# Attention and a routed expert layer on one core: new costs in the planner that orders the merge, and another path for two weight remainders

## The chip, the cores and the metric

The kernel runs on one core of one Trainium2 chip. The metric is the device time of one execution in microseconds (us). Engines are named as in the profile: PE multiplies matrices, DVE and ACT work on vectors, POOL issues the indirect and the adding transfers, SP issues plain transfers.

## The reference

Windowed attention (8 batches, 8 heads, 576 positions, head size 64, window 64) gives 4608 tokens of 512 numbers. Tokens are then assigned greedily to 8 experts of at most 576 tokens each, by all token-expert scores in falling order, and every expert is a two-layer product:

```python
logits = x @ w_gate
for idx in np.argsort(-logits.flatten()):
    tok, e = (int(idx) // E, int(idx) % E)
    if assigned[tok] >= 0 or counts[e] >= cap:
        continue
    assigned[tok] = e
    counts[e] += 1
...
    h = np.maximum(x[mask] @ w1[e], 0.0)
    out[mask] = h @ w2[e]
```

## The kernel before, in words

The first part, up to about 150 us, is the attention (`attention`), which writes the tokens `xs` to HBM and the gate scores to `L`. The change does not touch it.

The second part, the merge, runs two chains side by side. **Routing** (`Routing.steps`, L536) goes through the experts one after the other. A pass for expert p makes every token's best choice (`choices`, L490, six DVE operations), copies the choices on ACT into `one4` (L557), searches the score of the last token that still fits in 8 rounds (DVE compares L514, a count on PE L593, then some ten small DVE operations L602 to L663), and writes the list of the expert's tokens (L704 to L774: scan, PE products L707 and L756 and L768, the index tile `idx` L774). After the list, DVE updates the state for the next pass (L779 to L807). **Products** (`Experts.steps`, L984) are PE's bulk: for each expert a first layer (L1021), of 16 units with 12 matmuls, and a second (L1054 and L1064). Numbers are split in a rounded part and a remainder, so a matrix product takes three matmuls (wh by xh, wl by xh, wh by xl).

Between the two stands `turn` (L938): as soon as `idx` of expert p is there, POOL issues five gathers (L957; four of 128 tokens, one of 64) into `xg`, and PE transposes the tiles (L975) into two PSUM buffers; ACT copies each to `xh` (L946), DVE makes the remainder `xl` (L950) and frees the buffer. A transposed expert can start its first layer.

Weights come in eight chunks of 512 KB per expert (`load`, L865): SP (for the first expert's last four chunks POOL, L877) fetches a chunk into `st`; ACT rounds it to `wh` (L900). The remainder `wl` is made either by a DVE subtraction (L906; `quick`, L931: the first expert's chunks 0, 1, 2 and the last weights of all), or by an ACT copy of -wh (L911) and an adding transfer that POOL issues (L913), which adds `st` onto it.

The order of the instructions on each engine is not written by hand. `Streams` (L1072) is a planner that runs when the program is built: every chain is a generator that issues instructions and yields the time after which it may go on. `busy(dt, eng)` (L1084) books time on an engine and returns when the booking ends. What is issued first in planned time stands first in the engine's queue, and an engine takes its queue in order. So a wrong cost shows as an engine waiting for another. The costs of the DVE chain are booked by

```python
def dve(self, dt):
    return self.busy(0.4 * dt, "dve") + 0.6 * dt
```

so 40% of a step occupies DVE. ACT isn't booked at all. The transposes of expert p are planned from the gathers: `there` = now + POOL's booking (6400 ns) + GATHER, 2900 ns for the first expert and 6500 ns for the others, and tiles (0, 1), (2, 3), (4) come 3840, 1280 and 0 ns before it; from the third expert on they also wait for the next counting product of the routing, or at most JOIN ns. In the first round of a pass, PE's count waits 3500 ns of planned time after the ACT copies (L558).

Of the kernel before, what the change touches and what calls it, by code (L numbers as in the profile page):

```python
# [10 lines left out]
FT = mybir.dt.float32  # L11
# [5 lines left out]
OP = mybir.AluOpType  # L17
# [381 lines left out]
class Routing:  # L399
# [132 lines left out]
    def dve(self, dt):  # L532

        return self.busy(0.4 * dt, "dve") + 0.6 * dt

    def steps(self, p):  # L536
# [7 lines left out]
        if p < E - 1:  # L544
# [19 lines left out]
            for r in range(NR):  # L564
# [4 lines left out]
                if not p:  # L569
# [8 lines left out]
                    yield self.dve(1350)  # L578
                else:
                    c4 = self.room(128, 72)  # L580
                    cn, c4 = c4[:, 64:72], c4[0:M, 0:4 * ND]
                    for j0, j1 in ((0, 20), (20, 36)):
                        self.compare(G, thr, j0, j1)
                        yield self.dve(420)
                    for f in rest:
                        f()
                    yield self.dve(200) + slack
# [18 lines left out]
                    yield self.dve(450)  # L606
# [4 lines left out]
                    yield self.dve(400)  # L611

                step = float(1 << 28 - 4 * r) if r else 1.0
                if own:
# [4 lines left out]
                    yield self.dve(400)  # L619
# [5 lines left out]
                    yield self.dve(400) + slack  # L625
# [41 lines left out]
                yield self.dve(400)  # L667
            for f in rest:
                f()
            yield self.dve(200)  # L670
# [11 lines left out]
            yield self.dve(600)  # L682
# [8 lines left out]
            yield self.dve(600)  # L691
        else:
# [7 lines left out]
            yield self.dve(800)  # L700
# [4 lines left out]
        yield self.dve(250) + (600 if p else 0)  # L705
# [7 lines left out]
                                       op0=OP.add, op1=OP.mult)  # L713
        si = tile_([128, 3, NJ], I32, name="si")
        nc.vector.scalar_tensor_tensor(si[:, 0], Y[:, 0], -1.0, Y[:, 1], op0=OP.add, op1=OP.add)
        yield self.dve(500)
# [4 lines left out]
        yield self.dve(500)  # L721
# [18 lines left out]
        yield self.dve(410)  # L740
        nc.scalar.activation(Rw[:, 0], pairs(A_), AF.Copy, scale=self.lane)
        if p:
            nc.vector.tensor_tensor(Bw, pairs(self.r32), sb[:, 1].rearrange("p (q h) -> p q h", h=2)[:, None]
                                    .to_broadcast([128, 32, NJ // 2, 2]), OP.is_equal)
            yield self.dve(1200)
        for j0, j1 in ((0, NJ),) if p else ((0, 18), (18, 36)):
# [5 lines left out]
            yield self.dve(600) + slack + (500 if p else 0)  # L752
# [7 lines left out]
            yield self.busy(n * (18 if p else 29) + (90 if p else 0))  # L760
        yield self.dve(200) + slack
        ils = tile_([72, 32, 2], BF, name="ils")
        nc.vector.tensor_copy(ils.rearrange("p a h -> p (a h)"), il[0:72])
        yield self.dve(300)
# [7 lines left out]
        yield self.busy(100) + 200 + slack  # L772
        idx = self.rt.tile([128, 5], U32, name=f"idx{p}")
        nc.vector.tensor_copy(idx, ip)  # L774
        self.idx[p] = idx
        yield self.dve(200)
        if p < E - 1:
            if not p:
                nc.vector.scalar_tensor_tensor(self.eid, m, T[:, 0:1], best, op0=OP.is_gt, op1=OP.mult)  # L779
            eq = tile_([128, NJ], FT, name="eq")  # L780
            nc.vector.scalar_tensor_tensor(eq, Y[:, 1], CAP + 0.5, X[:, 1], op0=OP.is_lt, op1=OP.mult)
            nc.vector.scalar_tensor_tensor(self.eid, eq, code[:, 0:1], self.eid, op0=OP.mult, op1=OP.add)
            nc.vector.tensor_scalar(self.un, self.eid, 0.0, None, op0=OP.is_equal)
            yield self.dve(400)
            e1 = tile_([128, E], FT, name="e1")
            nc.vector.tensor_scalar(e1, self.cw, code, -FAR, op0=OP.is_equal, op1=OP.mult)
            nc.vector.tensor_tensor(V, V, e1[:, None, :].to_broadcast([128, NJ, E]), OP.add)
            yield self.dve(600)

            nc.vector.scalar_tensor_tensor(self.oh, m[:, :, None].to_broadcast([128, NJ, E]), T[:, 0:1], one,  # L790
                                           op0=OP.is_gt, op1=OP.mult)
            c2 = tile_([128, E], BF, name="c2")
            with nc.allow_low_precision(reason="whole numbers up to 36"):
                nc.vector.tensor_reduce(c2, self.oh.rearrange("p j e -> p e j"), axis=AX.X, op=OP.add)
            e2 = tile_([128, E], FT, name="e2")
            nc.vector.tensor_scalar(e2, self.cw, code, -1.0e6, op0=OP.is_equal, op1=OP.mult)
            nc.vector.tensor_tensor(self.left, self.left, e2, OP.add)
            if 0 < p < E - 2:
                self.kept = c2
                yield self.dve(1100)  # L800
                return
            yield self.dve(1100) + (slack if p < OWN else 1500)
            cn = self.room(128, E)
            nc.tensor.matmul(cn, self.ones, c2, start=True, stop=True)
            self.joined()
            yield self.busy(110) + 200 + slack
            nc.vector.tensor_tensor(self.left, self.left, cn, OP.add)  # L807
            yield self.dve(200)
# [21 lines left out]
class Experts:  # L830
# [34 lines left out]
    def load(self, p, ei):  # L865
# [26 lines left out]
        for i in range(2 * NCH):  # L892
# [8 lines left out]
            yield 1050  # L901
# [3 lines left out]
            if quick:  # L905
                nc.vector.tensor_tensor(lo, st[i], hi.bitcast(FT), OP.subtract)  # L906
                dt = self.busy(1130, "dve")
                self.spawn(self.ready(p, i, hi, lo), dt + 300 if p else 0)
            else:

                nc.scalar.activation(lo, hi.bitcast(FT), AF.Copy, scale=-1.0)  # L911
                yield 1150
# [18 lines left out]
    def quick(self, p, i):  # L931
        return p == 0 and i < 3 or p * 2 * NCH + i >= (E - 2) * 2 * NCH + NCH
# [5 lines left out]
    def turn(self, p, idx):  # L938
# [4 lines left out]
        def evac(a, n, t):  # L943
# [4 lines left out]
            yield 700  # L948
# [6 lines left out]
        for a in range(5):  # L955
# [3 lines left out]
            self.busy(TOKENS, "dma")  # L959
        self.gathered += 1  # L960
        there = self.clock() + self.busy(6400, "pool") + GATHER[p > 0]
# [4 lines left out]
        for tiles in ((0, 1), (2, 3), (4,)) if p else ((0,), (1,), (2,), (3,), (4,)):  # L966
            yield max(0, there - 1280 * (4 - tiles[-1]) - self.clock())
            if p > 1:

                n0, t0 = self.joins, self.clock() + JOIN[tiles[0] // 2]  # L970
                yield lambda: self.routed or self.joins > n0 or self.clock() >= t0
            for n, a in enumerate(tiles):
# [3 lines left out]
                dt = self.busy(260)  # L976
# [7 lines left out]
    def steps(self, p, idx):  # L984
# [6 lines left out]
        def evac(f, c0, h):  # L991
            c1 = c0 + h.shape[1]
            nc.scalar.activation(hh[:, f, c0:c1], h, AF.Relu)  # L993
            yield 500
# [34 lines left out]
        self.first += 1  # L1029

        def put(a, o):
            ot = fw.tile([128, DM], FT, name="ot", bufs=3)
            m = 128 if a < 4 else 64
            if a < 4:
                nc.scalar.activation(ot, o, AF.Copy)  # L1035
            else:
                t = fw.tile([64, DM], FT, name="low")
                nc.scalar.activation(t, o[64:128], AF.Copy)
                yield 650
# [67 lines left out]
def body(tc, q, k, v, vt, wg, w1, w2, xs, out):  # L1107
    nc = tc.nc
    with ExitStack() as ctx:
# [17 lines left out]
        def route():  # L1127
            for p in range(E):
                for dt in rt.steps(p):
# [3 lines left out]
                    if p in rt.idx and p not in listed:  # L1133
                        listed.add(p)
                        st.add(ex.turn(p, rt.idx[p]))
                    yield dt
            ex.routed = True
# [6 lines left out]
        known, listed = set(), set()  # L1144
# [20 lines left out]
```

## Time and profile before

| | us |
|---|---|
| median of 3 runs (lowest, highest) | 650.95 (649.75, 651.98) |
| the profiled execution, its own time | 650.87 |
| its span, first to last instruction | 648.9 |
| PE busy (share of the span) | 611.3 (94%) |
| DVE busy | 454.1 (70%) |
| ACT busy | 346.1 (53%) |
| POOL busy | 186.2 (29%) |

The page's slices show the attention up to about 150 us, a stretch with PE nearly idle around 150 to 180 us (the first routing pass, with no product to cover it), and then PE at 9 or more tenths up to the end. Where an engine's row carries a bracket, it gives the idle time before the instruction and what ended it. PEclk is the granted share of TensorE's full clock of 2.4 GHz; 0.5 is 1.2 GHz.

### The profile page before, as it was taken

To read this page: it belongs to the slowest core of one execution; us is meant where nothing else is said; L and a number is where in the kernel's file an instruction comes from. 1 tells how busy PE (TensorE), PEld (TensorE's weight loads), DVE (VectorE), ACT (ScalarE), POOL (GpSimd) and SP (SyncE) were. 2 spreads that over 40 slices of the span, in tenths; PEclk is the share of its full clock that TensorE was granted. 3 is DMA by queue.
4 is the path that set the end of the run, shared out by engine and by line. 5 is a ranking of instruction groups with operands and counts; after the bars stand their busy time and mean duration, and the time that the engine had idled before them with its cause. 6 is when DMAs were issued, how large, how long until landed. Compare 5 with 4: busy or idle time off the path is not lost.

```text
span 648.9 us, 16904 instructions
## 1 busy us (share of the span) xinstructions
PE 611.3 (94%) x6375; PEld 532.0 (82%) x6375; DVE 454.1 (70%) x2126; ACT 346.1 (53%) x724; POOL 186.2 (29%) x242
## 2 busy tenths in 40 slices
PE   8899999994599999999899999999999999999996
PEld 6677778884389879978797898899789879989985
DVE  7788888886789868876786787688678755523300
ACT  6798999980265176337526643572664354524210
POOL 1334353331141162026105411620541164011011
PEclk9999999996599998999899999999999999999999
DMA  9999999931376199459918964991896399411001
GB/s 313 373 367 368 371 385 368 336 109 36 130 237 130 30 315 240 82 195 218 234 21 300 246 120 149 247 242 30 295 248 122 124 273 321 153 36 38 1 25 48
DMA packets 44657, 127.81 MB, mean 197 GB/s; under 512 B 4632, under 2 KB 5272, under 8 KB 44576
## 3 DMA queue, kind: packets, MB, share of 16 engines
q1 hardware_dynamic: 30736, 79.52, 34.1%
q0 software_dynamic: 13552, 46.69, 30.8%
q8 instruction: 50, 0.82, 0.5%
q10 hardware_dynamic: 288, 0.52, 0.3%
q14 instruction: 31, 0.25, 0.1%
HBM read 82.15 MB, written 18.87 MB: 156 GB/s over the span
## 4 chain that ended last, share of the span: by engine, by line
PE 49%; issue 20%; POOL 4%; DMA 2%; ACT 1%; DVE 0%; POOLq 0%; ACTq 0%
PE h L1021 22%; PE o L1064 18%; PE o L1054 3%; POOL out L1043 2%; PE rps L593 2%; DMA wl<-st 1%; PE tp L975 1%; POOL xg L957 1%; DMA xg<-xs,idx 1%; POOL wl L913 1%; PE rps L756 1%; ACT wh L900 0%; ACT wl L911 0%; PE rps L758 0%; POOLq L1161 0%
## 5 line engine op out<-in xcount | busy, mean ns | idle before, releaser
L1043 POOL DMA_INDIRECT out<-ot,idx x40 | 40.4, 1010 | 252.8 <-ACT ot L1035 87.8
L993 ACT ACTIVATE hh<-h 128x256 fp32r<-128x256 f32 (+1 forms) x128 | 52.4, 409 | 110.3 <-PE h L1021 109.0
L1064 PE MATMUL o<-wh,hh 128*128 128x512 f32 x256 | 101.4, 396 | 0.0
L1064 PE MATMUL o<-wh,hl 128*128 128x512 f32 x256 | 100.8, 394 | 0.0
L1064 PE MATMUL o<-wl,hh 128*128 128x512 f32 x256 | 100.5, 393 | 0.0
L141 ACT ACTIVATE pe<-st,mx 128x128 f32<-128x128 f32 x288 | 92.0, 393 | 5.8 <-DVE mx L136 5.5
L1021 PE MATMUL h<-xh,wh 128*128 128x256 f32 (+1 forms) x512 | 93.0, 302 | 1.7 <-issue 0.9
L1021 PE MATMUL h<-xl,wh 128*128 128x256 f32 (+1 forms) x512 | 93.4, 300 | 0.0
L998 DVE SCALAR_TENSOR_TENSOR hl<-h,hh 128x256 fp32r<-128x256 f32 x128 | 53.6, 419 | 56.5 <-ACT hh L993 55.9
L1021 PE MATMUL h<-xh,wl 128*128 128x256 f32 (+1 forms) x512 | 91.9, 299 | 0.0
L1021 PEld LDWEIGHTS h<-xh,wh 128*128 128x128 f32 x512 | 76.8, 192 | 2.8 <-ACT xh L946 1.4
L1021 PEld LDWEIGHTS h<-xh,wl 128*128 128x128 f32 x512 | 76.7, 192 | 0.0
L1021 PEld LDWEIGHTS h<-xl,wh 128*128 128x128 f32 x512 | 76.6, 192 | 0.0
L900 ACT ACTIVATE wh<-st 128x1024 fp32r<-128x1024 f32 x64 | 67.3, 1052 | 2.7 <-DMA st<-w 2.5
L136 DVE CUSTOM_DVE_ANT_0 st<-Sp,mask 128x128 f32<-128x128 f32 x288 | 63.7, 285 | 5.7 <-PE Sp L128 5.2
L913 POOL DMA_DIRECT2D wl<-st x49 | 44.6, 976 | 68.9 <-ACT wl L911 25.9
L1035 ACT ACTIVATE ot<-o 128x512 f32<-128x512 f32 x32 | 19.1, 597 | 70.9 <-PE o L1064 63.2
L1064 PEld LDWEIGHTS o<-wh,hl 128*128 128x128 f32 x256 | 48.1, 188 | 9.6
L1064 PEld LDWEIGHTS o<-wl,hh 128*128 128x128 f32 x256 | 48.1, 188 | 9.3
L1064 PEld LDWEIGHTS o<-wh,hh 128*128 128x128 f32 x256 | 48.1, 188 | 9.3
L911 ACT ACTIVATE wl<-wh 128x1024 fp32r<-128x1024 f32 x49 | 51.8, 1056 | 0.6
L168 PE MATMUL Op<-VO,pt 128*64 128x73 f32 x640 | 45.3, 230 | 2.5 <-ACT pt L150 1.1
(182 smaller groups left out, 1093.2 us busy)
## 6 DMA issues: line engine op xcount, KB each, us to landing
st<-w SPq DMA_DIRECT2D x60, 512.0 KB
wl<-st POOLq DMA_DIRECT2D x49, 512.0 KB
xs<-x SPq DMA_DIRECT2D x36, 256.0 KB
VO<-v SPq DMA_DIRECT2D x6, 1168.0 KB
Q<-q SPq DMA_DIRECT2D x6, 1152.0 KB
K<-k SPq DMA_DIRECT2D x6, 1152.0 KB
VT<-vt SPq DMA_DIRECT2D x6, 1152.0 KB
VO<-v SPq DMA_DIRECT2D x4, 584.0 KB
```

Of the source, the lines that this page charges most:

```text
L136: nc.vector.tensor_tensor_reduce(st[:, h, :], Sp[h % 2][:, h // 2], mk, scale=-0.125, scalar=3.0e38, op0=OP.add, op1=OP.min, accum_out=mx[ ...
L141: nc.scalar.activation(pe[:, h, :], st[:, h, :], AF.Exp, bias=mx[:, h:h + 1], scale=-1.0)
L168: nc.tensor.matmul(Op[64 * a:64 * a + 64, g, h, :], pt[:, h, 64 * a:64 * a + 64], vv[a][:, 4 * g + h, :], start=True, stop=True)
L900: nc.scalar.activation(hi, st[i], AF.Copy)
L911: nc.scalar.activation(lo, hi.bitcast(FT), AF.Copy, scale=-1.0)
L913: nc.gpsimd.dma_start(lo.bitcast(FT), st[i], accum_op=OP.add)
L993: nc.scalar.activation(hh[:, f, c0:c1], h, AF.Relu)
L998: nc.vector.scalar_tensor_tensor(t, h[:, a - c0:b - c0], 0.0, hh[:, f, a:b].bitcast(FT), op0=OP.max, op1=OP.subtract)
L1021: nc.tensor.matmul(h, wv[:, cc, 128 * (f % 2):128 * (f % 2) + 128], xt[:, cc, c0:c1], start=(k == 0), stop=(k == 11))
L1043: nc.gpsimd.indirect_dma_start(out=self.out[5 * p + a], out_offset=IndirectOffsetOnAxis(ap=idx[0:m, a:a + 1], axis=0), in_=ot[0:m], in_off ...
L1054: nc.tensor.matmul(o, hh[:, f, 512:], w[:, 512 * (f % 2):512 * (f % 2) + 512], start=(f == 0 and n == 0), stop=(f == NF - 1 and n == 1))
L1064: nc.tensor.matmul(o, ht[:, f, 128 * a:128 * a + 128], wt[:, 512 * (f % 2):512 * (f % 2) + 512], start=(k == 0), stop=(k == 23))
```

## The change

It does four things. First, `dve(dt, n)` books `dt - 110 n` on DVE, where n counts the operations of the step, and nearly every step gets a new dt; ACT's copies are booked on an engine "act". Second, several fixed waits go or shrink: after the ACT copies the first count waits until the booked copies end plus 200 ns, in place of 3500 (300 for the second expert); the scan's wait of 600 ns and 500 ns at L752 go. Third, the transposes are planned by GATHER = 4200 for all experts, and the JOIN wait is cut off at a time counted from the start of the expert's second layer (SECOND). Fourth, of the first expert's weights only chunk 0 keeps the DVE subtraction, which is issued 2600 ns after the gathers; chunks 1 and 2 get the ACT copy and the adding transfer; and POOL issues the fetches of chunks 4, 5, 6 together after chunk 2. The list (L715 to L774) becomes a function `listing`, in the same place of the pass. `turn` is started where `idx` is issued.

```diff
-    def dve(self, dt):
-        return self.busy(0.4 * dt, "dve") + 0.6 * dt
+    def dve(self, dt, n=1):
+        return self.busy(dt - 110 * n, "dve") + 110 * n
...
-                yield 3500 if p > 1 else 300
+                copied = self.clock() + self.busy(1260, "act") + 200
...
-                        yield self.dve(420)
+                        yield self.dve(480 - 4 * j0)
...
-                    yield self.dve(200) + slack
+                    if r:
+                        self.dve(360, 2)
+                    yield max(slack, copied - self.clock() if own and not r else 0)
...
-                    yield self.dve(450)
+                    yield self.dve(530, 2) + (150 if kept is not None else 0)
...
-                    yield self.dve(400)
+                    yield self.dve(490, 2)
...
-                    yield self.dve(400)
+                    yield self.dve(440, 2)
...
-                    yield self.dve(400) + slack
+                    yield self.dve(430, 2)
...
-        yield self.dve(250) + (600 if p else 0)
+        yield self.dve(340) + slack
...
-            yield self.dve(600) + slack + (500 if p else 0)
+            yield max(self.dve(810 if p else 740, 1 if p else 2) + slack, lanes - self.clock())
...
-GATHER = (2900, 6500)
+GATHER = 4200
...
-JOIN = (800, 2000, 3300)
+JOIN = ((800, -1800), (2000, 900), (3300, 2000))
+SECOND = 27500
...
-            if quick:
+            if p == 0 and i == 0:
+                self.spawn(self.subtract(i, hi, lo, st[i]), max(0, self.begun + 2600 - self.clock()))
+                dt = 1200
+            elif quick:
...
-            if i + ahead < 2 * NCH:
-                fetch(i + ahead)
-            yield max(100, dt - 1200) if p or i < 3 else 900
+            for n in () if p == 0 and i < 2 else (4, 5, 6) if p == 0 and i == 2 else (i + ahead,):
+                if n < 2 * NCH:
+                    fetch(n)
+            yield max(100, dt - 1200) if p or i < 1 else 900
...
-        return p == 0 and i < 3 or p * 2 * NCH + i >= (E - 2) * 2 * NCH + NCH
+        return p == 0 and i < 1 or p * 2 * NCH + i >= (E - 2) * 2 * NCH + NCH
...
-        there = self.clock() + self.busy(6400, "pool") + GATHER[p > 0]
+        there = self.clock() + self.busy(6400, "pool") + GATHER
...
-                n0, t0 = self.joins, self.clock() + JOIN[tiles[0] // 2]
+                n0, (t0, t1) = self.joins, JOIN[tiles[0] // 2]
+                t0 = min(self.clock() + t0, self.started + SECOND + t1)
```

## Rows read from the trace of the kernel before

**Rows 1.** Busy time by stretch (us, instructions of PE, PEld, DVE, ACT, POOL), PEclk, DMA share, GB/s
```profile
176.00:240.60 64.60, 63.32 (x459) 54.92 (x458) 53.36 (x199) 32.89 (x51) 22.23 (x25) 0.98 0.64 185
240.60:249.00 8.40, 6.48 (x54) 6.20 (x53) 5.99 (x21) 6.84 (x11) 4.16 (x5) 0.80 1.06 198
...
302.40:316.50 14.10, 11.29 (x87) 10.74 (x88) 10.73 (x43) 9.26 (x15) 3.67 (x4) 0.88 1.05 249
...
341.00:398.00 57.00, 57.00 (x427) 50.89 (x426) 43.82 (x178) 29.10 (x47) 17.35 (x19) 1.00 0.72 190
...
512.00:540.00 28.00, 26.88 (x181) 21.23 (x180) 14.73 (x44) 14.97 (x21) 13.01 (x15) 1.00 0.97 278
```

**Rows 2.** Timeline of PE: transposes, first products, waits (start, length, instruction, idle before)
```profile
240.64 0.79 PE L975 MATMUL tp<-identr,xg 128*128 128x128 f32 x8
...
242.71 0.53 PE L975 MATMUL tp<-identr,xg 128*128 128x128 f32 x4 [0.98 <-DVE xl L950]
244.18 0.72 PE L975 MATMUL tp<-identr,xg 128*128 128x128 f32 x4 [0.94 <-PE tp L975]
...
302.69 0.74 PE L1021 MATMUL h<-xh,wh 128*128 128x256 f32 x4 [0.32 <-ACT xh L946]
...
310.47 0.59 PE L593 MATMUL rps<-G,one 128*128 128x60 bf16 x9 [2.05 <-DVE G L514]
...
358.43 0.86 PE L975 MATMUL tp<-identr,xg 128*128 128x128 f32 x8
...
365.90 0.64 PE L1021 MATMUL h<-xh,wh 128*128 128x256 f32 x4
...
533.19 0.23 PE L768 MATMUL rps<-s,ils 72*32 72x5 bf16 x8 [1.12 <-DVE ils L763]
```

**Rows 3.** Timeline of DVE: the index tile of the second, third and fourth expert
```profile
232.26 0.17 DVE L774 CAST idx<-rps 128x5 uint32<-128x5 f32 x1 [0.73 <-PE rps L768]
...
289.55 0.16 DVE L774 CAST idx<-rps 128x5 uint32<-128x5 f32 x1 [0.74 <-PE rps L768]
...
347.94 0.17 DVE L774 CAST idx<-rps 128x5 uint32<-128x5 f32 x1 [0.73 <-PE rps L768]
```

**Rows 4.** Timelines of ACT, PE, DVE: first round of the fourth expert's routing
```profile
295.06 1.34 ACT L557 COPY one<-one 128x384 bf16<-128x384 bf16 x3
...
299.80 0.42 PE L593 MATMUL rps<-G,one 128*128 128x60 bf16 x9
...
300.26 0.16 DVE L599 TENSOR_TENSOR st<-st,rps 128x8 f32<-128x8 f32 x1 [4.53 <-PE rps L593]
```

**Rows 5.** Timelines of DVE, POOL, ACT around the first expert's gathers
```profile
177.46 1.23 DVE L906 TENSOR_TENSOR wl<-st,wh 128x1024 fp32r<-128x1024 f32 x1
...
181.37 1.22 DVE L906 TENSOR_TENSOR wl<-st,wh 128x1024 fp32r<-128x1024 f32 x1
182.51 0.44 DVE L499 TENSOR_REDUCE m<-L 128x36 f32<-128x288 f32 x1
...
177.70 1.81 POOL L957 DMA_INDIRECT xg<-xs,idx  x1 [0.31 <-issue]
...
182.43 0.96 POOL L957 DMA_INDIRECT rest<-xs,idx  x1 [0.30 <-issue]
...
182.15 0.60 ACT L946 ACTIVATE xh<-tp 128x512 fp32r<-128x512 f32 x1 [3.04 <-PE tp L975]
```

**Rows 6.** An adding transfer on POOL, its DMA by 1 us, a long one in the chain
```profile
193.96 0.88 POOL L913 DMA_DIRECT2D wl<-st  x1 [6.20 <-ACT hh L993]
...
194.00:195.00 1.00, 1.00 (x10) 1.00 (x9) 0.90 (x6) 0.55 (x2) 0.83 (x1) 1.00 0.01 4
195.00:196.00 1.00, 1.00 (x16) 0.89 (x14) 1.00 (x3) 0.97 (x2) 0.00 (x0) 1.00 0.68 131
...
198.00:199.00 1.00, 1.00 (x9) 1.00 (x8) 0.86 (x5) 0.74 (x3) 0.05 (x1) 1.00 0.51 94
...
310.36 9.29 DMA wl<-st
```

**Rows 7.** Timeline of PE: the first expert's first use of wl of chunks 1 and 2
```profile
188.64 0.64 PE L1021 MATMUL h<-xh,wl 128*128 128x256 f32 x4
...
191.86 0.64 PE L1021 MATMUL h<-xh,wl 128*128 128x256 f32 x4
```

More of the change, by code (lines that the diff above doesn't have):

```diff
@@ L713, in steps @@
                                        op0=OP.add, op1=OP.mult)
+        yield self.dve(260)
+        yield from self.listing(p, Y, slack)
+        if p < E - 1:
+            if not p:
+                nc.vector.scalar_tensor_tensor(self.eid, m, T[:, 0:1], best, op0=OP.is_gt, op1=OP.mult)
+            eq = tile_([128, NJ], FT, name="eq")
+            nc.vector.scalar_tensor_tensor(eq, Y[:, 1], CAP + 0.5, X[:, 1], op0=OP.is_lt, op1=OP.mult)
+            nc.vector.scalar_tensor_tensor(self.eid, eq, code[:, 0:1], self.eid, op0=OP.mult, op1=OP.add)
+            nc.vector.tensor_scalar(self.un, self.eid, 0.0, None, op0=OP.is_equal)
+            yield self.dve(750, 4 - (p > 0))
+            e1 = tile_([128, E], FT, name="e1")
+            nc.vector.tensor_scalar(e1, self.cw, code, -FAR, op0=OP.is_equal, op1=OP.mult)
+            nc.vector.tensor_tensor(V, V, e1[:, None, :].to_broadcast([128, NJ, E]), OP.add)
+            yield self.dve(730, 2)
+            nc.vector.scalar_tensor_tensor(self.oh, m[:, :, None].to_broadcast([128, NJ, E]), T[:, 0:1], one,
+                                           op0=OP.is_gt, op1=OP.mult)
+            c2 = tile_([128, E], BF, name="c2")
+            with nc.allow_low_precision(reason="whole numbers up to 36"):
+                nc.vector.tensor_reduce(c2, self.oh.rearrange("p j e -> p e j"), axis=AX.X, op=OP.add)
+            e2 = tile_([128, E], FT, name="e2")
+            nc.vector.tensor_scalar(e2, self.cw, code, -1.0e6, op0=OP.is_equal, op1=OP.mult)
+            nc.vector.tensor_tensor(self.left, self.left, e2, OP.add)
+            if 0 < p < E - 2:
+                self.kept = c2
+                yield self.dve(1550, 3)
+                return
+            yield self.dve(1550, 3) + 300
+            cn = self.room(128, E)
+            nc.tensor.matmul(cn, self.ones, c2, start=True, stop=True)
+            self.joined()
+            yield self.busy(110) + 200 + slack
+            nc.vector.tensor_tensor(self.left, self.left, cn, OP.add)
+            yield self.dve(200)
@@ L771, in steps @@
             self.warm(28)
-        yield self.busy(100) + 200 + slack
+        yield self.busy(255) + 200 + slack
         idx = self.rt.tile([128, 5], U32, name=f"idx{p}")
         nc.vector.tensor_copy(idx, ip)
-        self.idx[p] = idx
+        self.listed(p, idx)
         yield self.dve(200)
[L777 to L808, printed above, removed]
     def expert(self, p, code):
@@ L900, in load @@
             nc.scalar.activation(hi, st[i], AF.Copy)
-            yield 1050
+            yield self.busy(1050, "act")
             quick = self.quick(p, i)
@@ L947, in evac @@
             self.tiles[p] = a + 1
-            yield 700
+            yield self.busy(520 if n > 64 else 300, "act") + 160
             self.busy(600, "dve")
@@ L959, in turn @@
             self.busy(TOKENS, "dma")
+        if not p:
+            self.begun = self.clock()
         self.gathered += 1
-        there = self.clock() + self.busy(6400, "pool") + GATHER[p > 0]
+        there = self.clock() + self.busy(6400, "pool") + GATHER
         yield lambda: self.first == p
@@ L1029, in steps @@
         self.first += 1
+        self.started = self.clock()
         def put(a, o):
@@ L1035, in put @@
                 nc.scalar.activation(ot, o, AF.Copy)
+                self.busy(500, "act")
             else:
@@ L1142, in products, with listed @@
                 yield from ex.steps(p, rt.idx[p])
-        known, listed = set(), set()
+        def listed(p, idx):
+            rt.idx[p] = idx
+            ex.routed = p == E - 1
+            st.add(ex.turn(p, idx))
+        known = set()
+        rt.listed, rt.spawn, rt.clock = listed, st.add, ex.clock
         st.add(route())
```

48 lines of the change are left out of this document (26 added, 22 removed).

## The prediction

> **What bounds the kernel now.** I read the busy times by stretch first. Between the merge's first product and its end PE is the bound: from 341 to 398, a whole period, it is busy for 57.00 of 57.00 us at the full clock [rows 1]. No instruction of the products goes or comes, so the change can only gain where PE stands still or runs at 1.2 GHz. In the stretches of [rows 1] after the start these are three:
>
> - Where the second expert takes over (240.6 to 249): idle 8.40 - 6.48 = 1.92 us, and a granted clock of 0.80 costs (1 - 0.80) x 8.4 = 1.68. Together 3.60.
> - Where the third takes over (302.4 to 316.5): 14.10 - 11.29 = 2.81 idle and 0.12 x 14.1 = 1.69 of clock. Together 4.50.
> - At 532: 28.00 - 26.88 = 1.12 idle.
>
> The sum, 9.2 us, is the most that better order can return here. The idle 1.28 us before 240.6 lie mostly at the start of the first expert, behind its gathers, and I leave them.
>
> Then the timelines, for the cause. In the first place PE transposes tiles 0 and 1 only at 240.64, when nothing of the first expert is left to run, and tiles 2 and 3 wait 0.98 and 0.94 us for the two PSUM buffers, which DVE frees after xl [rows 2]. In the second, PE waits 2.05 us for a DVE compare that the planner thought done [rows 2]. At 533.19 it waits 1.12 for the list's copy on DVE [rows 2]. In all three PE's queue holds an instruction ahead of its time. The index tiles say why the later experts have no such place: idx came 240.6 - 232.26 = 8.3 us before the end of the running second layer for the second expert, 302.4 - 289.55 = 12.9 for the third, and 365.9 - 347.94 = 18.0 for the fourth, whose transposes stand at 358.43, inside the products, without a wait [rows 2, 3]. Routing starts late and catches up over two experts, while PE pays.
>
> **The change part by part.**
>
> *GATHER.* The first pair of transposes was planned 6.40 + 6.50 - 3.84 = 9.06 us after idx; in the trace it came 240.64 - 232.26 = 8.4 after [rows 2, 3]. It becomes 6.76. So it moves 2.3 us forward, into the second layer, where the wait for PSUM runs beside matmuls. If the tokens haven't landed by then, PE waits for them; POOL issues the second tile's gather within 2.7 us of idx at about 1.0 each [rows 5], which leaves 4 us for its landing. Cost nothing; without that cover PE stands for what is missing, up to 2.3 us.
>
> *Waits of the routing pass.* In the fourth expert's pass the ACT copies ended at 295.06 + 1.34 = 296.40, PE's first count ran at 299.80, and DVE sat idle 4.53 us for it [rows 4]. The new wait is the copies plus 0.2 us; I take 2.4 us off each pass (bounds 0 if another step is late next, 3.4 if none is), and 0.4 for the waits of the list. Next late is DVE itself.
>
> *The second expert's pass.* Two subtractions of 1.22 leave DVE; the pass began at 182.51, right behind the last of them (181.37 + 1.22) [rows 5]. I take 1.5 us (bounds 0 and 2.4). So idx of the second expert comes near 232.3 - 1.5 - 0.4 = 230.4, its first transposes at 237.2, 3.4 us before the end of the layer, and of the 3.60 us I take 3.2 back. The third expert's pass took 289.55 - 232.26 = 57.3 us [rows 3]; 57.3 - 2.8 = 54.5 puts its idx at 284.9, against an end at 302.4 - 3.2 = 299.2: 14.3 us, and with transposes 2.3 earlier this is as good as 16.6 was. That is nearer to the fourth expert's 18.0 (no loss) than to the third's 12.9 (4.50), so I take 4.0 of the 4.50.
>
> *True DVE and ACT costs.* They decide where PE's counts stand. More DVE time booked puts counts later, so PE should no longer meet a compare that isn't done. Of the 1.12 at 532 I take half, 0.6: the copy there stood behind a remainder that waited for ACT, and ACT is now booked. In the experts where PE is full this costs nothing as long as idx keeps its lead.
>
> *Adding transfers for chunks 1 and 2.* Removed: 2 x 1.22 on DVE. Added: two ACT copies of about 1.05, which fit in ACT's idle 3.04 us before 182.15 [rows 5]; two issues of 0.88 on POOL [rows 6], behind the five gathers, so from 183.4 at the latest (182.43 + 0.96) [rows 5]; two transfers. The three fetches of chunks 4 to 6 move behind them, some 2 us later; those chunks are first used in the second layer, so nobody waits. For the landing, the transfer issued alone at 193.96 began to move after 195 and was done by 198.5: 4.5 us from issue, 3.3 of them moving [rows 6]. Chunk 1 lands at 183.4 + 4.5 = 187.9 and chunk 2 behind it at 191.2. PE wants them at 188.64 and 191.86 [rows 7]. That is 0.7 us to spare for both. The other bound is the chain's 9.29 us for such a transfer beside full DMA queues [rows 6]: chunk 1 at 192.7, 4.1 late, plus a fall of the clock like those above, 1.7: 5.8. I take 0.3, since the DMA engines have little else there, and keep 0 and 5.8.
>
> *The first subtraction later.* The gather that was issued at 177.70, inside the subtraction of 177.46 to 178.69, took 1.81 us in place of about 1.0 and ended 0.8 after it [rows 5]. Three gathers near 541 to 545 that met a subtraction show the same. Moved by 2.6 us after the gathers' start, the subtraction meets the third gather or none. If none, all later POOL work starts 0.85 us sooner; if the third, nothing is won. I take nothing: chunk 0's remainder is wanted only at the first expert's fifth matmul, and the end of the gathers hides it.
> The Trainium skill (SBUF — State Buffer, section on the two separate sides) gives a rule for this: a DVE operation with two SBUF inputs and a GpSimd operation exclude each other for a whole instruction, and the later one blocks. The slow gather agrees with it. By that rule the moved subtraction would still block whatever POOL starts within its 1.2 us, so that the two adding transfers would start up to 0.4 (1.22 less 0.85) later than by the sum above and use half of their 0.7 to spare. The sum would stay as it is.
>
> **Sum.** 3.2 + 4.0 + 0.6 - 0.3 = 7.5 us. The profiled execution took 650.87, with 2.0 outside its span, and lies 0.08 under the median; 650.87 - 7.5 = 643.4.
>
> **The rivals.**
> 1. *Only one place is mended.* The third expert's idx comes too late still, because DVE and not the waits sets the pass (it is busy 43.82 of 57 us while PE is full [rows 1], and more in the first layers). Then the 4.0 stay lost: 647.4. For it: passes of 57.3 and 58.4 us [rows 3] show no reserve. Against: the idle 4.53 on DVE inside such a pass [rows 4].
> 2. *The first expert waits for chunk 1.* At the far bound the loss is 5.8: 650.87 - 7.8 + 5.8 = 648.9. For it: 0.7 us of reserve, and a queue that also holds gathers. Against: the transfer measured with the DMA engines free.
> 3. *Slower: the routing pass becomes the bound.* With true costs the planner books more DVE time, so each step of the 8 rounds may be issued later; a pass that comes out longer than the products' 57.0 us loses its lead at every expert. The loss starts when idx comes less than about 13 to 16 us before the end of a second layer; at 3.6 to 4.5 a place [rows 1], and two to six places in place of two, this gives 651 to 667; I take 658, four places (two more of 3.6). For it: PE's period and the pass are equal within 1.4 us. Against: the waits that go, 2.8 us a pass.
> 4. *The order hardly changes*, because booked costs and real ones differ by tenths: 650.9.
>
> **How the numbers follow.** Forecast 0.66; rival 1 gets 0.12, rival 2 gets 0.06, rival 3 gets 0.10, rival 4 gets 0.06. About 0.3%, 2 us, is what a measurement of this kernel can tell from no change: faster means under 649.0. Forecast and rival 1 are faster, rival 2 lies half on either side of that bound: 0.66 + 0.12 + 0.03 = 0.81. Same: 0.06 + 0.03 = 0.09. Slower: 0.10. The low end is all 9.2 us and nothing lost at the start, 641.7, and 0.85 from gathers that end sooner: 640.8. The high end takes in rivals 1 and 2: 649.0. What is left out is rivals 3 and 4 and little else.
>
> **What would show it.** Right: in the stretches at the second and third expert's start PE has no idle time over 0.5 us and the clock stays at 1.0; the transposes of tiles 0 and 1 stand between L1064 matmuls; idx of the second expert near 230 and of the third near 285; DVE's wait before L599 is about 2 us; L913 for chunk 1 stands behind the last gather, near 183, and PE shows no wait for it at the first expert's third unit. Wrong: idle PE before a wl of chunk 1 or 2 (rival 2), idle PE before L593 or L975 at several experts' starts (rival 3), or an idx that keeps its place (rivals 1 and 4).

## The result, and the profile after

The changed kernel took 646.09 us (median of 10 runs, 643.70 to 649.02) beside 652.50 for the kernel before on the same chip: a ratio of 0.9909, 95% interval 0.9887 to 0.9931, so 0.9% or about 6 us faster (4.5 to 7.4). One of the ten executions of the kernel before took 982.09 us, and the ratio leaves it out. A second timing (e9, below) gave 0.9906 (0.9878 to 0.9933). The prediction was 643.4 us, 7.5 less than before, with a range of 640.8 to 649.0.

The profiled execution took 649.02 us (span 647.4). Its first expert's idx came at 181.03, against 175.94 in the kernel before: the attention, which has no edit, ended 5.4 us later there (its last DVE operation began at 156.47, against 151.08), and the first routing pass was 0.3 us shorter. So I compare the **merge**, from the first expert's idx to the end of PE's last product: 467.05 us before, 460.27 after, 6.8 less. The two ends of the merge, in the timelines of DVE and PE, kernel before:

```profile
175.94 0.17 DVE L774 CAST idx<-h 128x5 uint32<-128x5 f32 x1 [0.35 <-PE h L768]
...
642.60 0.39 PE L1064 MATMUL o<-wh,hl 128*128 128x512 f32 x1
```

After, from DVE and PE too, with the index tiles of the first four experts (L816 is the old L774; transposes are now L998, the first layer L1044, the second L1079 and L1089, counts L595, wl by subtraction L939, by transfer L927):

```profile
181.03 0.17 DVE L816 CAST idx<-h 128x5 uint32<-128x5 f32 x1 [0.35 <-PE h L810]
...
238.40 0.17 DVE L816 CAST idx<-rps 128x5 uint32<-128x5 f32 x1 [0.40 <-PE rps L810]
...
293.11 0.17 DVE L816 CAST idx<-rps 128x5 uint32<-128x5 f32 x1 [0.74 <-PE rps L810]
...
347.07 0.17 DVE L816 CAST idx<-rps 128x5 uint32<-128x5 f32 x1 [0.57 <-PE rps L810]
...
640.91 0.39 PE L1089 MATMUL o<-wh,hl 128*128 128x512 f32 x1
```

Busy times by stretch after, cut to answer to [rows 1] (the second expert's takeover, the third's, the end of the lists):

```profile
249.10:257.50 8.40, 7.98 (x74) 7.48 (x73) 7.17 (x30) 6.74 (x13) 2.94 (x4) 1.00 1.03 220
307.00:321.00 14.00, 14.00 (x122) 13.82 (x121) 12.76 (x54) 10.80 (x18) 3.65 (x4) 1.00 1.05 249
504.40:532.40 28.00, 27.34 (x183) 21.82 (x182) 15.50 (x46) 15.29 (x21) 15.62 (x17) 1.00 0.88 246
```

At both takeovers PE is busy but for the 0.42 us below, and its clock stays at 1.00. The timeline of PE after shows why, beside [rows 2]: the transposes stand ahead of the last L1089 products, and the first layer follows them without a wait; one wait of 0.42 us, for a weight remainder, is left.

```profile
245.45 0.93 PE L998 MATMUL tp<-identr,xg 128*128 128x128 f32 x8
246.22 0.46 PE L1089 MATMUL o<-wl,hh 128*128 128x512 f32 x1
...
248.52 0.80 PE L998 MATMUL tp<-identr,xg 128*128 128x128 f32 x8
249.15 0.70 PE L1044 MATMUL h<-xh,wh 128*128 128x256 f32 x4
250.27 0.74 PE L1044 MATMUL h<-xh,wl 128*128 128x256 f32 x4 [0.42 <-DMA wl<-st]
...
301.35 0.85 PE L998 MATMUL tp<-identr,xg 128*128 128x128 f32 x8
...
306.48 0.85 PE L998 MATMUL tp<-identr,xg 128*128 128x128 f32 x8
307.16 0.71 PE L1044 MATMUL h<-xh,wh 128*128 128x256 f32 x4
```

Not all of it is gain. In the first expert's first layer a new wait stands, and the queues of ACT and DVE after name its cause (one timeline each of PE, ACT, DVE, in this order):

```profile
195.00 0.50 PE L998 MATMUL tp<-identr,rest 128*128 128x128 f32 x4 [1.46 <-DVE pq L618]
...
189.18 1.05 ACT L911 ACTIVATE wh<-st 128x1024 fp32r<-128x1024 f32 x1
190.13 1.32 ACT L557 COPY one<-one 128x384 bf16<-128x384 bf16 x3
191.36 1.06 ACT L925 ACTIVATE wl<-wh 128x1024 fp32r<-128x1024 f32 x1
192.32 0.58 ACT L966 ACTIVATE xh<-tp 128x512 fp32r<-128x512 f32 x1
...
193.13 0.22 DVE L604 TENSOR_TENSOR dg<-rps,diag 128x60 f32<-128x60 f32 x1 [2.29 <-PE rps L595]
...
194.06 0.68 DVE L970 TENSOR_TENSOR xl<-tp,xh 128x512 fp32r<-128x512 f32 x1
```

The fifth tile's transpose needs a PSUM buffer that the xl of the third tile frees (194.06 to 194.74; the bracket names the small DVE operation right behind it). Two queues delay that xl: ACT makes chunk 3's two halves (189.18, 191.36) and, between them, the copies of the choices ahead of the tile's xh, and on DVE the routing's first count (dg, waiting for PE, and three small operations) stands ahead of it. In the kernel before chunk 3's halves stood there too, but ACT's queue had the copies of the choices behind the last tile:

```profile
183.86 1.05 ACT L900 ACTIVATE wh<-st 128x1024 fp32r<-128x1024 f32 x1
184.94 1.06 ACT L911 ACTIVATE wl<-wh 128x1024 fp32r<-128x1024 f32 x1
185.91 0.58 ACT L946 ACTIVATE xh<-tp 128x512 fp32r<-128x512 f32 x1
...
188.65 0.38 ACT L946 ACTIVATE xh<-tp 128x256 fp32r<-128x256 f32 x1 [0.27 <-PE tp L975]
188.93 1.33 ACT L557 COPY one<-one 128x384 bf16<-128x384 bf16 x3
```

The pass that two subtractions no longer delay has moved in among the tokens.

The merge in parts, from starts in the timelines: *layer 1* is the first expert's first L1044 to its first second-layer product; *period 1* from there to the second expert's first second-layer product (it holds the second's takeover), *period 2* one expert on. *From product 1* is the merge without its start, from the first L1044 to the end. The starts in the timelines of PE, kernel before and then the changed kernel:

```profile
184.02 0.74 PE L1021 MATMUL h<-xh,wh 128*128 128x256 f32 x4 [0.86 <-issue]
...
212.70 0.40 PE L1054 MATMUL o<-wh,hh 128*128 128x512 f32 x1
...
274.11 0.39 PE L1054 MATMUL o<-wh,hh 128*128 128x512 f32 x1
...
336.96 0.39 PE L1054 MATMUL o<-wh,hh 128*128 128x512 f32 x1
```

```profile
189.34 0.74 PE L1044 MATMUL h<-xh,wh 128*128 128x256 f32 x4 [1.23 <-ACT xh L966]
...
219.86 0.39 PE L1079 MATMUL o<-wh,hh 128*128 128x512 f32 x1
...
278.12 0.39 PE L1079 MATMUL o<-wh,hh 128*128 128x512 f32 x1
...
334.92 0.40 PE L1079 MATMUL o<-wh,hh 128*128 128x512 f32 x1
```

| kernel | layer 1 | period 1 | period 2 | merge | from product 1 | time (before, same chip) |
|---|---|---|---|---|---|---|
| before | 28.68 | 61.41 | 62.85 | 467.05 | 458.97 |  |
| after | 30.52 | 58.26 | 56.80 | 460.27 | 451.96 | 646.09 (652.50) |
| e1 transposes as before | 29.97 | 62.09 | 60.92 | 466.70 | 458.22 | 650.53 (653.36), one run |
| e2 wait of 3500 back | 30.95 | 57.81 | 56.83 | 460.04 | 451.26 | 644.22 (653.36), one run |
| e3 three subtractions | 28.78 | 59.76 | 57.21 | 460.77 | 452.04 | 644.29 (653.36), one run |
| e4 chunk 3 later | 29.15 | 58.35 | 57.01 | 459.31 | 450.52 | 645.15 (653.36), one run |
| e5 transposes alone | 30.78 | 58.35 | 56.84 | 458.65 | 450.98 | 642.02 (650.16), one run |
| e6 old costs | 31.43 | 58.82 | 57.58 | 461.90 | 453.93 | 647.39 (650.16), one run |
| e7 adding transfers alone | 30.09 | 58.08 | 64.01 | 465.89 | 457.43 | 650.23 (650.16), one run |
| e8 transposes alone, not first expert's | 28.85 | 60.67 | 56.85 | 461.03 | 452.53 | 644.84 (652.43) |
| e9 after again | 30.61 | 58.34 | 56.80 | 461.04 | 452.21 | 645.14 (652.43) |
| e10 chunk 3 later, timed | 28.85 | 58.30 | 56.86 | 458.85 | 450.04 | 643.13 (652.43) |
| e11 transposes alone, timed | 30.91 | 58.26 | 56.85 | 458.53 | 450.98 | 644.19 (650.05) |
| e12 chunk 3 later, timed | 28.95 | 58.16 | 56.79 | 457.72 | 449.95 | 642.78 (650.05) |

Before to after, the differences sum to the 6.8: start to first product +0.23 (8.08 to 8.31), layer 1 +1.84, period 1 -3.15, period 2 -6.05, the three later periods +0.47, the rest -0.12. Kernels that ran more than once agree in the merge within 1.6 us (e4, e10, e12) or better (after and e9: 0.8; e5 and e11: 0.1), and from product 1 on within 0.6 (0.57, 0.25 and 0.00): most of the spread is the start, so the last but one column tells two kernels apart better. Times of single runs vary more, with the attention's end.

### The profile page after: what moved, and what is told of

The parts are those of the page before. It is cut to its first block, busy times and chain, and to the rows that moved or that the text cites. A ratio compares the mean times of both kernels' runs of the same rounds, so it can differ in the third digit from the quotient of the medians.

```text
span 647.4 us, 16906 instructions
## 1 busy us (share of the span) xinstructions
PE 610.8 (94%) x6375; PEld 531.4 (82%) x6375; DVE 450.2 (70%) x2124; ACT 349.5 (54%) x726; POOL 186.8 (29%) x244
## 4 chain that ended last, share of the span: by engine, by line
PE 52%; issue 19%; POOL 2%; DMA 2%; ACT 1%; DVE 0%; POOLq 0%; ACTq 0%
PE h L1044 24%; PE o L1089 19%; PE o L1079 3%; PE rps L595 2%; PE tp L998 2%; POOL out L1068 2%; DMA wl<-st 1%; DMA xg<-xs,idx 1%; PE rps L798 1%; POOL xg L977 0%; ACT R L782 0%; PE rps L800 0%; PE rps L810 0%; POOLq L1188 0%; ACT xh L966 0%
## 5 line engine op out<-in xcount | busy, mean ns | idle before, releaser
L1089 PE MATMUL o<-wh,hh 128*128 128x512 f32 x256 | 101.0, 395 | 0.0
L1089 PE MATMUL o<-wl,hh 128*128 128x512 f32 x256 | 100.9, 394 | 0.0
L1089 PE MATMUL o<-wh,hl 128*128 128x512 f32 x256 | 100.5, 393 | 0.0
L1044 PE MATMUL h<-xh,wh 128*128 128x256 f32 (+1 forms) x512 | 92.6, 299 | 1.2 <-ACT xh L966 1.2
L1044 PE MATMUL h<-xh,wl 128*128 128x256 f32 (+1 forms) x512 | 91.5, 298 | 0.4 <-DMA wl<-st 0.4
L1044 PE MATMUL h<-xl,wh 128*128 128x256 f32 (+1 forms) x512 | 91.9, 298 | 0.0
L1044 PEld LDWEIGHTS h<-xh,wh 128*128 128x128 f32 x512 | 75.9, 189 | 1.8 <-ACT xh L966 1.4
L1044 PEld LDWEIGHTS h<-xh,wl 128*128 128x128 f32 x512 | 75.7, 190 | 0.6 <-DMA wl<-st 0.6
L1044 PEld LDWEIGHTS h<-xl,wh 128*128 128x128 f32 x512 | 76.0, 190 | 0.0
L927 POOL DMA_DIRECT2D wl<-st x51 | 46.2, 990 | 65.0 <-ACT wl L925 37.9
L1089 PEld LDWEIGHTS o<-wh,hl 128*128 128x128 f32 x256 | 48.1, 188 | 9.6
L1089 PEld LDWEIGHTS o<-wh,hh 128*128 128x128 f32 x256 | 48.1, 188 | 9.4
L1089 PEld LDWEIGHTS o<-wl,hh 128*128 128x128 f32 x256 | 48.1, 188 | 9.3
L925 ACT ACTIVATE wl<-wh 128x1024 fp32r<-128x1024 f32 x51 | 53.9, 1057 | 0.7
```

The source lines that it names most:

```text
L1044: nc.tensor.matmul(h, wv[:, cc, 128 * (f % 2):128 * (f % 2) + 128], xt[:, cc, c0:c1], start=(k == 0), stop=(k == 11))
L1089: nc.tensor.matmul(o, ht[:, f, 128 * a:128 * a + 128], wt[:, 512 * (f % 2):512 * (f % 2) + 512], start=(k == 0), stop=(k == 23))
```

## The experiments

**e1, e5, e11, e8: the transposes.** First the changed kernel with the transposes planned as before:

```diff
-GATHER = 4200
+GATHER = (2900, 6500)
-                t0 = min(self.clock() + t0, self.started + SECOND + t1)
+                t0 = self.clock() + t0
```

> The changed kernel with the transposes planned as before (GATHER 2900 and 6500, JOIN without the cut-off). Measured from the first expert's index tile on DVE to PE's last matmul, the merge takes 467.0 us before the change and 460.3 after it. Theory T (the earlier transposes mend the takeovers): the stall where the second expert takes over comes back, idle plus clock near 3 us, and the merge takes 463 to 466. Rival P (the shorter routing passes mend them, the transposes only follow): merge within 1 us of 460.3.

The merge was 466.70, within 0.35 of the kernel before and 0.7 above theory T's range; periods 1 and 2 are long again (62.09, 60.92). At the takeovers PE now waits, in its timeline of e1, for the xh of tile 1, which stands on ACT behind a chunk's two copies (243.32, 244.74; the bracket names the second), and for the compares:

```profile
246.34 1.01 PE L1044 MATMUL h<-xh,wh 128*128 128x256 f32 x3 [2.92 <-ACT wl L925]
...
312.40 0.31 PE L595 MATMUL rps<-G,one 128*128 128x60 bf16 x5 [1.53 <-DVE G L514]
```

So without the earlier transposes the other three parts return next to nothing (0.35 in the merge, 0.75 from product 1 on). The other way round, the transposes alone in the kernel before:

```diff
-GATHER = (2900, 6500)
+GATHER = 4200
-JOIN = (800, 2000, 3300)
+JOIN = ((800, -1800), (2000, 900), (3300, 2000))
+SECOND = 27500
...
-                n0, t0 = self.joins, self.clock() + JOIN[tiles[0] // 2]
+                n0, (t0, t1) = self.joins, JOIN[tiles[0] // 2]
+                t0 = min(self.clock() + t0, self.started + SECOND + t1)
```

> The kernel before with the earlier transposes alone (GATHER 4200 for all, JOIN with its cut-off). Merge before 467.0 us, changed kernel 460.3, changed kernel with late transposes 466.7. Theory T1 (the transposes alone carry the gain): both takeovers clean, merge 459.5 to 461.5. Rival T2 (they need the true costs beside them, else PE's counts stand ahead of DVE's compares again): the second expert's takeover is clean, the third keeps its 2 us wait for a compare and the clock's fall, merge 462 to 465.

The merge fell to 458.65, below T1's range and the changed kernel's, and both takeovers are clean; the lead of routing needs neither the new costs nor the shorter waits. GATHER and the cut-off of JOIN were not tried apart; the second expert's transposes have no JOIN wait, so there GATHER alone does it. Timed:

> The kernel before with the earlier transposes alone, timed. Its one look gave a merge of 458.65 us, 1.6 below the changed kernel's first. Theory: the transposes carry the whole gain, and the other three parts together are worth nothing or less; then it lies 7 to 10 us below the kernel before, and within 1 us of the changed kernel with chunk 3 late. Rival: the look was a lucky execution; then it lies with the changed kernel itself, 6.5 to 7.5 us below before and 1.5 to 2.5 above the one with chunk 3 late.

0.9917 (0.9884 to 0.9950), 5.9 us below before, 1.4 above e12 on the same chip: nearer to the rival, and outside both lists of numbers. The merge was 458.53, so e5's had not been luck. In time the transposes alone give about what the whole change gives; the difference is too small for these intervals. From product 1 on they give more: 450.98 twice, beside 451.96 and 452.21 for the changed kernel.

In e5 PE waited in the first expert (timelines of PE and DVE of e5): the xl of tile 1 stood behind the choices, since GATHER = 4200 is *later* than the 2900 that the first expert had.

```profile
186.13 0.39 PE L1023 MATMUL h<-xl,wh 128*128 128x256 f32 x1 [1.41 <-DVE xl L951]
...
185.02 0.46 DVE L506 TENSOR_TENSOR one<-w,best 128x288 bf16<-128x288 bf16 x1
185.39 0.68 DVE L951 TENSOR_TENSOR xl<-tp,xh 128x512 fp32r<-128x512 f32 x1
```

So e8 keeps 2900 there: `GATHER = (2900, 4200)`, all else as e5.

> The kernel before with the earlier transposes (and the cut-off of their wait) for the second and later experts alone; the first expert keeps 2900 ns. In the kernel with them for all experts PE waited 1.41 us at 186.13 for xl of tile 1, and its first layer took 30.78 us from first product to first second-layer product, against 28.68 before. Theory F: the first expert's later transposes did that, by putting its xl behind DVE's choices; then the first layer is back at 28.5 to 29.2 us, the wait of 1.41 is gone, the periods are about 58.4, 56.8 and 57.0 as there, and the merge is 456 to 457.5 us, below both kernels (467.05 before, 460.27 after). Rival: it is only the order that happens to come out, and the first layer stays at 30 or more; then the merge is 458 to 460.5.

Layer 1 is back at 28.85 and the wait gone, as theory F had it, but the merge was 461.03: period 1 grew from 58.35 to 60.67. PE's timeline of e8 shows part of the 2.3 us:

```profile
244.79 0.50 PE L1023 MATMUL h<-xh,wl 128*128 128x256 f32 x2 [0.90 <-DMA wl<-st]
...
249.05 0.31 PE L593 MATMUL rps<-G,one 128*128 128x60 bf16 x5 [0.53 <-DVE G L514]
249.69 0.27 PE L593 MATMUL rps<-G,one 128*128 128x60 bf16 x4 [0.33 <-DVE G L514]
```

PE now comes to the second expert before that expert's weights and before the compares are done. The theory of the place was right, that of the sum wrong (461.03 lies above the rival's range too): what layer 1 wins is lost at the next late thing. These waits are 1.76 us, where e5 has 0.33 in this place, so they make 1.4 of the 2.3; the rest I did not settle.

**e2: the waits of the routing pass.** The changed kernel with the old wait after ACT's copies:

```diff
-                copied = self.clock() + self.busy(1260, "act") + 200
+                self.busy(1260, "act")
+                yield 3500 if p > 1 else 300
+                copied = self.clock()
```

> The changed kernel with the fixed wait of 3500 (300 for the second expert) between the ACT copies and the first count put back. Theory T: passes grow from about 54.9 to about 57 us, but the takeovers stay clean, merge within 1 us of 460.3. Rival P: the third expert's index tile comes too late again and PE stalls there, merge 463 to 466.

The merge was 460.04, against 460.27. The last three full passes went back to 56.9 us (idx to idx), yet no expert waited for them. The third expert's pass took 54.28, although its first count was read 10.75 us after idx for 8.87: it made that up. The shorter wait buys lead that nobody needs.

**e6: the costs.** The changed kernel with the old booking:

```diff
-        return self.busy(dt - 110 * n, "dve") + 110 * n
+        return self.busy(0.4 * dt, "dve") + 0.6 * dt
...
+        if eng == "act":
+            return dt
```

> The changed kernel with the old booking (40% of a DVE step, nothing on ACT) under the new numbers. Theory T1: no takeover returns, merge 459.5 to 461.5. Rival T2: PE waits over 1 us for compares (L595 on G) at the second or third expert, merge 462 to 465.

461.90: 1.6 more than the changed kernel's first profile and 0.9 more than its second (e9), between the two theories; from product 1 on, where equal kernels agree within 0.6, it is 2.0 and 1.7 more. PE's timeline of e6 has waits for compares that the changed kernel doesn't have, 1.7 us in three places:

```profile
196.67 0.27 PE L595 MATMUL rps<-G,one 128*128 128x60 bf16 x4 [1.11 <-DVE G L514]
...
247.82 0.27 PE L595 MATMUL rps<-G,one 128*128 128x60 bf16 x4 [0.18 <-DVE G L514]
...
316.27 0.59 PE L595 MATMUL rps<-G,one 128*128 128x60 bf16 x9 [0.40 <-DVE G L514]
```

**e3, e7: the adding transfers.** The changed kernel with DVE's subtraction for chunks 0 to 2, the first of them at its old place, and the old order of fetches:

```diff
-            if p == 0 and i == 0:
-                self.spawn(self.subtract(i, hi, lo, st[i]), max(0, self.begun + 2600 - self.clock()))
-                dt = 1200
-            elif quick:
+            if quick:
...
-            for n in () if p == 0 and i < 2 else (4, 5, 6) if p == 0 and i == 2 else (i + ahead,):
+            for n in (i + ahead,):
...
-        return p == 0 and i < 1 or p * 2 * NCH + i >= (E - 2) * 2 * NCH + NCH
+        return p == 0 and i < 3 or p * 2 * NCH + i >= (E - 2) * 2 * NCH + NCH
```

> The changed kernel with DVE subtractions for the first expert's chunks 0, 1 and 2 and the fetches in their old order. Theory A (the adding transfers relieve DVE at the start, as the prediction had it): the second expert's index tile comes 1 to 2.5 us later, merge 461 to 463. Rival B (at the start DVE waits for PE and ACT, not for itself, so the two subtractions are free, and the ACT copies of chunks 1 to 3 are what delays xh): first layer of the first expert back from 30.5 to about 28.7 us, merge 458 to 460.

460.77, between A and B: layer 1 is 1.74 shorter (28.78) and period 1 is 1.50 longer (59.76). The second expert's index tile is not later, as A had it (57.11 us after the first, for 57.37); PE comes to the takeover sooner and waits 1.19 us there, for 0.42. So the adding transfers cost in the first layer what they save at the takeover. Alone in the kernel before (the same lines the other way round):

> The kernel before with the adding transfers for the first expert's chunks 1 and 2 alone (later subtraction of chunk 0 and fetches with it). Theory A (it frees DVE and brings the second expert's index tile forward): pass of 54 to 55.5 in place of 56.3, first takeover partly mended, merge 464 to 466. Rival B (it only lengthens the first layer, from 28.7 to 29.5 or more, and the index tile keeps its place): merge 467 to 469.

650.23 beside 650.16, merge 465.89: in A's range, with B's longer first layer (30.09) and a pass of 55.96, hardly shorter than 56.32. The second's takeover was mended (58.08), but the third's became worse (64.01, with a compare that PE waited 2.05 us for at 309.49, as at 310.47 before [rows 2]).

**e4, e10, e12: chunk 3 behind the tokens.** If the 1.46 us wait at 195.00 hangs on ACT's queue, it goes when chunk 3's halves, the part of it that can wait, may start only after the fifth tile:

```diff
-                yield lambda: self.tiles[0] > 1
+                yield lambda: self.tiles[0] > 4
```

> The changed kernel with one number changed: the first expert's chunk 3 is rounded on ACT only after all five token tiles (tiles > 4 in place of > 1). Theory: in the changed kernel PE's 1.46 us wait before the last transpose at 195.0 comes from ACT, whose queue holds chunk 3's two copies ahead of xh of tile 2, so that DVE makes xl of tile 2 only behind the routing's first counts. Then the wait goes, merge 458.5 to 459.5. Rival (the routing's first count itself is too early, whatever ACT does): the wait stays over 1 us and the merge is 460 to 461.

Layer 1 29.15, merge 459.31, and the wait gone. Timed beside the changed kernel (e9), and again beside e11:

> The changed kernel as it is, beside the others on one chip, so that their times can be compared. Merge 459.5 to 461.5 us as in its first profile (460.27); time 5 to 7 us under the kernel before.

> The changed kernel with the halves of chunk 3 behind the first expert's tokens, timed. In one look its merge was 459.31, 1.0 below the changed kernel's, since the 1.46 us wait for PSUM at 195 was gone. If that holds, 0.5 to 1.5 us below the changed kernel on this chip; the rival is that the order varies by as much from one execution to the next, and the two times then lie within 0.4 us of each other.

> The changed kernel with the halves of chunk 3 behind the tokens, timed on the same chip as the transposes alone. It was 9.3 us below the kernel before in the timing beside the changed kernel; the same here, 8.5 to 10, if that holds.

e9: 0.9906, 7.3 us below before, a little more than expected, merge 461.04. e10: 0.9884 (0.9843 to 0.9925), 9.3 below before and 2.0 below e9, more than the 0.5 to 1.5 expected; its merge is 2.2 less. e12: 0.9893 (0.9860 to 0.9925), 7.3 below before, short of the expected 8.5, with the shortest merge of all (457.72). By its medians it is the best kernel here, below before and after; its interval and the changed kernel's overlap, so for the 2 us the merges speak more clearly than the times: from product 1 on the three runs take 449.95 to 450.52, the changed kernel's two 451.96 and 452.21.

e10 also answers whether the adding transfers land in time, since nothing delays its first layer once it has begun. Its timelines of POOL and PE: issue, then the first use of the remainders of chunk 1 (190.39) and chunk 2 (193.27), without a wait. (In e12 the uses come sooner, 6.09 and 8.97 us after the issue at 182.28, and don't wait either.)

```profile
183.29 1.95 POOL L927 DMA_DIRECT2D wl<-st  x2
...
190.39 0.64 PE L1044 MATMUL h<-xh,wl 128*128 128x256 f32 x4
...
193.27 0.64 PE L1044 MATMUL h<-xh,wl 128*128 128x256 f32 x4
```

## Why the prediction was right, and where not

The time fell inside the range, and the forecast's cause, transposes out of the gap and into the second layer, was the right one (e1, e5). The lead that it expected from shorter passes was not needed (e2, e5). The terms:

- **Second takeover, 3.2: measured 3.15, for half the reason given, and the rest luck.** The transposes came 245.45 - 238.40 = 7.05 us after idx (6.76 predicted) and 3.70 before the end of the layer (3.4 predicted). But the pass was to shrink from 56.3 to 54.4 and took 238.40 - 181.03 = 57.37. It began 1.3 us sooner after idx (L499 at 186.32, 5.29 after, for 182.51 - 175.94 = 6.57), and its first count was read 4.0 us sooner (dg: 12.1 for 16.05); by the second count nothing was left (20.23 for 20.21). The token tiles' work on DVE and the 1.46 us stop had moved between them. With the stop gone it is 55.23 to 56.47 (e4, e10, e12), still not 54.4: two subtractions less on DVE do not shorten the pass by their time. The takeover was clean all the same because PE reached it later: the start and layer 1 took 2.07 us more. Where layer 1 stays short and idx comes about 57 us after the first (57.11 in e3, 56.89 in e8), PE waits 1.19 and 1.76 us and period 1 is 59.76 and 60.67. Layer 1 and period 1 together returned 1.31, where the sum had 2.9.
- **Third takeover, 4.0: measured 6.05.** Mis-sized, because the most that it could return was taken from one stretch (4.50 us of idle time and clock in [rows 1]). By the lengths of the periods the place cost 62.85 - 56.95 = 5.9. The shorter pass was right in size (54.71 for 54.5) and not the cause: with the transposes alone the pass took 56.38 and the period was as short (56.84). Nor did the wait make that size, since the pass took 54.28 with the old wait back (e2); the match is luck.
- **Waits of the pass, 2.4 a pass.** L599's wait in the fourth expert's pass fell as predicted, from 4.53 to 2.27 us, and the first count was read 1.20 us after the copies' end for 3.86, as the timelines of ACT, PE and DVE after show beside [rows 4] (the bracket names a product, but the count ended last, at 301.51); but it was worth nothing by itself (e2).

```profile
299.03 1.32 ACT L557 COPY one<-one 128x384 bf16<-128x384 bf16 x3
...
301.09 0.42 PE L595 MATMUL rps<-G,one 128*128 128x60 bf16 x9
...
301.55 0.16 DVE L601 TENSOR_TENSOR st<-st,rps 128x8 f32<-128x8 f32 x1 [2.27 <-PE o L1089]
```

- **The 532 us wait, 0.6: measured about 0.1.** The wait of 1.12 went, and two of 0.27 and 0.39 came in its place at 523.06 and 524.11 (for the list's products), with one of 0.26 before a transpose at 566.63; the rest of the merge shortened by 0.12. The true costs, to which the prediction gave this term, are not needed for it: with the transposes alone (e5) the wait is gone too, and the rest takes 134.2 us, for 135.2 before and 135.1 after.
- **Adding transfers, 0.3 lost: the first layer lost 1.84.** The two ACT copies fitted into the idle time, as predicted (182.65 and 184.68 after, ahead of the first xh at 187.87), and the landing was in time: two transfers, issued at 183.29 in e10, for use at 190.39 and 193.27. The step that failed is the 1.5 us that leave DVE, taken as a gain of the pass alone: the pass came forward into the tokens' turn on ACT and DVE, and the first layer paid (e3: 1.74 back without it, e4: 1.37 back with ACT's queue relieved). Another term was left out: for the first expert GATHER rises from 2900 to 4200, which in the kernel before lengthened layer 1 by 1.9 us (30.78 in e5, 28.85 in e8); in the changed kernel's order e3, with the same 4200, has 28.78. The 1.46 us wait needs it as well: in e1, with 2900 for the first expert, it doesn't appear (layer 1 takes 29.97 there, at a granted clock of 0.88 in its first 14 us).
- **True costs, nothing outside 532: measured 0.9 to 1.6** in the merge, 1.7 to 2.0 from product 1 on (e6), and e8, which has the old costs, shows 0.86 us of such waits. A term left out. But the costs alone don't keep PE from an unfinished compare, as the prediction expected: in e1, which has them, PE waits 1.87 us for compares at the third takeover (1.53 and 0.34), and in e5, without them, not at all there.
- **The first subtraction later, nothing.** Right: the gathers of the first expert now take 0.92 to 1.07 us each, 1.81 no more; they end 0.89 us sooner after idx (6.56 for 7.45), and their end was no bound. Timelines of POOL and DVE after, beside [rows 5]:

```profile
182.79 1.07 POOL L977 DMA_INDIRECT xg<-xs,idx  x1 [0.30 <-issue]
184.16 0.95 POOL L977 DMA_INDIRECT xg<-xs,idx  x1 [0.30 <-issue]
...
184.32 1.22 DVE L939 TENSOR_TENSOR wl<-st,wh 128x1024 fp32r<-128x1024 f32 x1 [0.23 <-DMA st<-w]
```

The rivals: 1 fell (the third's idx came in time), although its sign, an idx that keeps its place, did show at the second expert (57.37 after the first, 56.32 before); 2 fell (no wait for chunk 1 or 2); 3 fell (passes 54 to 55 us from the third expert on, no lead lost); 4 fell. That 6.8 lies so near to 7.5 is luck, since the errors nearly cancelled: the third takeover gave 2.05 more than its term, layer 1 1.54 less (1.84 for 0.3), the start 0.23, the 532 us wait 0.48 and the later periods 0.47 less, so that 7.5 became 6.8 in the merge.

What stays open: the first expert's first product comes 7.6 to 8.8 us after its idx, and in runs of one kernel as differently (8.81 in e10, 7.77 in e12). Part of this is the granted clock. In the routing pass ahead of it PE is not idle, but its clock is low: from 152 to 176 us it was busy 10.63 of 24.00 us at a clock of 0.50 (kernel before). About the time of idx it starts 28 products that nothing reads (L521), still at 0.50 (1.2 GHz). Where the clock rose early (e11: 0.64 in the first 2.5 us, 1.00 in the next 2.5) they took 4.44 us, and the first transpose came 5.32 after idx; where it rose late (e3: 0.50 in both) they took 6.04, and it came 6.49 after. From there to the first product it is another 2.2 to 3.2 us, and I did not find what sets that.

## What to carry to other kernels

Take the most that a place can return from the length of its period beside an undisturbed one, not from the idle time of a stretch chosen by eye. When work leaves an engine, follow what comes forward behind it and whom it now precedes: here the routing pass, 1.3 us sooner, stepped in front of the tokens in the queues of ACT and DVE. Parts of such a change don't add up: from product 1 on the transposes alone gave 8.0 us, all four parts together 7.0 and 6.8, so undo each by itself.

## What the chip showed that I had not expected

Which of a gather and a DVE subtraction starts first decides whether the gather is slow. Begun 0.24 us after a subtraction it took 1.81 us (177.70 after 177.46 [rows 5]); begun 0.16 before one (184.16 and 184.32, above) it took 0.95, and the subtraction its usual 1.22. In every run here a gather that began inside a subtraction ended 0.8 to 0.9 us after the subtraction's end: it took 2.09 us where it began 0.04 us after the subtraction's start (e5, 532.92), 1.57 where it began 0.46 after (e8, 182.07), and the usual 0.94 where it began 1.10 after (185.42 in the changed kernel). The Trainium skill (SBUF — State Buffer, section on the two separate sides) has the later of the two blocked whichever it is; the runs agree for a gather that comes later, and show no delay for a subtraction that does.
